# Replacing a hand-ordered attention and feed-forward kernel by a computed order, with w_in in growing chunks and transposes by DMA

## The chip, the cores and the metric

The kernel runs on one core of one Trainium2 chip. The metric is the time of one execution in microseconds (us), taken on the device. It is about 2 us longer than the span of the profile, which runs from the first to the last instruction (before: 236.56 us of time, 234.5 us of span). Each run carries a state, fast or slow; only fast runs are compared, and a profile of a slow run is marked where it is used.

## The reference

Linear attention with a decay per head, in blocks of 64 positions, then a feed-forward block on every token. Shapes: q, k, v are 4 x 8 x 768 x 64 (batch, heads, positions, width), float32; w_in is 512 x 2048, w_out 2048 x 512; the output is 3072 x 512.

```python
for b in range(nb):                                   # 12 blocks of 64 positions
    intra = np.einsum('bhic,bhjc->bhij', qb, kb) * Dmask[None]
    intra = np.einsum('bhij,bhjd->bhid', intra, vb)
    inter = np.einsum('bhid,bhde->bhie', qb * lam_pow[None], kv_state)
    out[:, :, sl] = intra + inter
    kv_state = lam_block[None, :, None, None] * kv_state + np.einsum('bhsd,bhse->bhde', kb_dec, vb)
...
h = x @ w_in
s = np.sin(alpha * h)
g = h + s * s / (alpha + 1e-09)
return (g @ w_out).astype(np.float32)
```

## The kernel before

The kernel cuts the attention into 24 units (256 positions of 4 heads of one batch). A unit loads three tiles of 256 KB (q, k, v), casts and scales them to bf16, transposes q and k on TensorE (eight 128x128 transposes), and then does on TensorE the scores, the masked output, the new states, and the product with the old state ("inter"). Four units make a group of 512 tokens. A group then costs 128 feed-forward matmuls of 128x512: 64 with w_in (tile `hps`, later `gall`) and 64 with w_out (tile `ops`, later `ob`). There are six groups.

The order is written by hand: eight units first, then the feed-forward of group 0, then units and feed-forward work mixed.

```python
    for u in range(8):
        load(u)                                  # SyncE: q, k, v of the first 8 units
    ...
    def group(g, tag):
        n0 = 4 * g
        okv = None
        for n in range(n0, n0 + 4):
            nxt = n + 1 < 8
            if nxt:
                scale_q(n + 1, V)
                scale_k(n + 1, G)
            if n >= WIN0 and n < WIN0 + WCH:     # WIN0 = 5: w_in waits for unit 5
                load_w_in(n - WIN0)
            okv = new_okv()
            if n > 0:
                intermm(n - 1, okv)
                outmm(n - 1, okv)
            scores(n)
            domask(n)
            kvmm(n, okv)
            ...
            if nxt:
                transposes(n + 1, tag, True)     # TensorE, for every unit
                cast_v(n + 1, A)
            busy(NB)                             # 4 dummy matmuls
    ...
    group(0, "hps")
    ...
    group(1, "hps")
    ...
    alone(NFC, hook0, (V, A, V, A, G, A, V, G))  # feed-forward of group 0
    alone(NPRE, hook1)
    ...
    for n in range(8, NU + 4):                   # steady stage: one unit, 8 blocks of 4 matmuls
        macro(n, 4 if n >= 12 else NFC // 4 - NPRE // 4, mid2, late2)
```

Of the kernel before, what the change touches and what calls it, by code (L numbers as in the profile page):

```python
# [12 lines left out]
ET = mybir.EngineType  # L14
# [3 lines left out]
def kernel(  # L18
# [24 lines left out]
    RING = 8  # L43
    WIN0 = 5
    GATE = 8
    N0 = 28
    NB = 4
    NPRE = 8
# [3 lines left out]
    wpool = ctx.enter_context(tc.tile_pool(name="wts", bufs=1))  # L52
    stagep = ctx.enter_context(tc.tile_pool(name="stage", bufs=RING))
    work = ctx.enter_context(tc.tile_pool(name="work", bufs=3))
    kvp = ctx.enter_context(tc.tile_pool(name="kv", bufs=2))
    xtp = ctx.enter_context(tc.tile_pool(name="xt", bufs=3))
    gbp = ctx.enter_context(tc.tile_pool(name="gb", bufs=3))
    mlps = ctx.enter_context(tc.tile_pool(name="mlps", bufs=3))
    outp = ctx.enter_context(tc.tile_pool(name="outp", bufs=3))
    PS = bass.MemoryType.PSUM  # L60
    ps = ctx.enter_context(tc.tile_pool(name="ps", bufs=1, space=PS))

    ctx.enter_context(tc.manual_schedule())


# [7 lines left out]
    BUFS = {"s0": 1, "s1": 1, "okv": 1, "hps": 3, "ops": 1}  # L73
    stage = {}

    def load(u, after=None):
        _, tp, b, _, hh = where(u)
        st = []
        for nm, src in (("q", q), ("k", k), ("v", v)):
            tl = stagep.tile([P, HH, 2, D], FP32, name=f"st_{nm}")  # L80
            ld = nc.sync.dma_start(  # L81
                out=tl[:].rearrange("p h two e -> p h (two e)"),
                in_=src[b, hh * HH:(hh + 1) * HH, tp * W:(tp + 1) * W, :]
                .rearrange("h (p two) e -> p h (two e)", two=2))
            if after is not None:
                tc.add_manual_dep(ld.ins, after.ins.name, mybir.DependencyInfo(
                    mybir.DependencyClass.Sync, mybir.DependencyReason.DATA))
                after = None
            st.append(tl)
        stage[u] = st  # L90

    zeros = consts.tile([P, 2 * P], BF16, name="zeros")
    nc.vector.memset(zeros[:], 0.0)
    warm = consts.tile([1, 1], FP32, name="warm")
    nc.vector.memset(warm[:], 0.0)  # L95
    nc.scalar.activation(out=warm[:], in_=warm[:], func=ACTF.Sin)
    lam_bc = consts.tile([P, H], FP32, name="lam_bc")
    nc.sync.dma_start(out=lam_bc[:], in_=lam.partition_broadcast(P))
    alpha_r = consts.tile([NFC, P], FP32, name="alpha_r")
    nc.scalar.dma_start(out=alpha_r[:], in_=moe_alpha.rearrange("(f p) -> f p", p=P))  # L100
    for u in range(8):
        load(u)

# [3 lines left out]
    for c in range(2):  # L107
        sl = slice(c * D, (c + 1) * D)
        nc.gpsimd.iota(out=pos[sl, :], pattern=[[0, 1]], base=1, channel_multiplier=2,
                       allow_small_or_imprecise_dtypes=True)  # L110
        nc.gpsimd.iota(out=jt[sl, :], pattern=[[1, 2]], base=0, channel_multiplier=2,
                       allow_small_or_imprecise_dtypes=True)
    it = consts.tile([P, 2, D], FP32, name="it")
    nc.gpsimd.iota(out=it[:], pattern=[[1, 2], [2, D]], base=0, channel_multiplier=0,
                   allow_small_or_imprecise_dtypes=True)
# [5 lines left out]
    nc.vector.tensor_tensor(  # L121
        out=mask[:], in0=it[:].rearrange("p two e -> p (two e)").unsqueeze(1)
        .to_broadcast([P, 2, 2 * D]),
        in1=jt[:].unsqueeze(2).to_broadcast([P, 2, 2 * D]), op=ALU.is_ge)
    E = consts.tile([P, 2, H], FP32, name="E")
    R = consts.tile([P, 2, H], FP32, name="R")
    nc.gpsimd.tensor_tensor(out=E[:, 0], in0=lam_bc[:], in1=pos[:].to_broadcast([P, H]),
                            op=ALU.pow)

    LT = consts.tile([P, H], FP32, name="LT")  # L130
    nc.vector.tensor_tensor(out=LT[:], in0=lam_bc[:], in1=lam_bc[:], op=ALU.mult)
    for i in range(6):
        nc.vector.tensor_tensor(out=LT[:], in0=LT[:], in1=LT[:], op=ALU.mult)
    nc.vector.tensor_tensor(out=E[:, 1], in0=E[:, 0], in1=lam_bc[:], op=ALU.mult)
    nc.vector.reciprocal(out=R[:], in_=E[:])
# [3 lines left out]
    w_in_sb = wpool.tile([P, NDC, DFF], BF16, name="w_in_sb")  # L139
    w_out_sb = wpool.tile([P, NFC, DM], BF16, name="w_out_sb")  # L140
    WCH = 4

    def load_w_in(j):
        w = DFF // WCH
        nc.gpsimd.dma_start(
            out=w_in_sb[:, :, j * w:(j + 1) * w],
            in_=moe_w_in[:, j * w:(j + 1) * w].rearrange("(c p) g -> p c g", p=P))

    def load_w_out(j):
        n = NFC // WCH  # L150
        nc.gpsimd.dma_start(
            out=w_out_sb[:, j * n:(j + 1) * n, :],
            in_=moe_w_out[j * n * P:(j + 1) * n * P, :].rearrange("(f p) d -> p f d", p=P))

    cast = {}

    def scale_q(u, eng):
        hh = where(u)[4]
        QL = work.tile([P, 2, HH, D], BF16, name="QL")
        hs = slice(hh * HH, (hh + 1) * HH)  # L160
        eng.tensor_tensor(out=QL[:], in0=stage[u][0][:].rearrange("p h two e -> p two h e"),  # L161
                          in1=E[:, :, hs].unsqueeze(3).to_broadcast([P, 2, HH, D]),
                          op=ALU.mult)
        cast[u, "q"] = QL

    def scale_k(u, eng):
        hh = where(u)[4]
        KD = work.tile([P, 2, HH, D], BF16, name="KD", bufs=4)
        hs = slice(hh * HH, (hh + 1) * HH)
        eng.tensor_tensor(out=KD[:], in0=stage[u][1][:].rearrange("p h two e -> p two h e"),  # L170
                          in1=R[:, :, hs].unsqueeze(3).to_broadcast([P, 2, HH, D]),
                          op=ALU.mult)
        cast[u, "k"] = KD

    def cast_v(u, eng):
        VB = work.tile([P, 2, HH, D], BF16, name="VB", bufs=4)
        v_in = stage[u][2][:].rearrange("p h two e -> p two h e")
        if eng is nc.scalar:
            nc.scalar.copy(out=VB[:], in_=v_in)  # L179
        else:  # L180
            eng.tensor_copy(out=VB[:], in_=v_in)
        cast[u, "v"] = VB

    qkt = {}

    def transposes(u, tag="s0", split=False):
        QT = work.tile([P, 2, 2, 2, P], BF16, name="QT")
        if split:
            pts = [ps.tile([P, 2, 2, P], BF16, name="pt", tag=tag, bufs=BUFS[tag])
                   for j in range(2)]  # L190
        else:
            pt = ps.tile([P, 2, 2, 2, P], BF16, name="pt", tag=tag, bufs=BUFS[tag])
            pts = [pt[:, 0], pt[:, 1]]
        for j, key in ((0, "q"), (1, "k")):
            for hp in range(2):
                for par in range(2):
                    nc.tensor.transpose(out=pts[j][:, hp, par, :],  # L197
                                        in_=cast[u, key][:, par, 2 * hp:2 * hp + 2, :],
                                        identity=iden[:])
        if split:  # L200
            nc.scalar.copy(out=QT[:, 1], in_=pts[1][:])  # L201
            nc.vector.tensor_copy(out=QT[:, 0], in_=pts[0][:])
        else:
            nc.scalar.copy(out=QT[:], in_=pt[:])  # L204
        qkt[u] = QT

    half = [slice(0, D), slice(D, 2 * D)]
    stm = {}
    sps = {}

    def scores(u):
        QT = qkt[u]
        sp = [ps.tile([P, 2, 2, P], FP32, name="sp", tag=f"s{hd}", bufs=1)
              for hd in range(2)]
        for hp in range(2):
            for par in range(2):
                for c in range(2):
                    for hd in range(2):
                        nc.tensor.matmul(  # L219
                            out=sp[hd][half[c], par, hp, :],  # L220
                            lhsT=QT[half[hd], 1, hp, par, half[c]],
                            rhs=QT[half[hd], 0, hp, :, half[c]],
                            start=True, stop=True)
        sps[u] = sp

    def domask(u):
        sp = sps.pop(u)
        ST = work.tile([P, 2, 2, 2, P], BF16, name="ST")
        for hd in range(2):
            nc.vector.tensor_tensor(  # L230
                out=ST[:, hd], in0=sp[hd][:],
                in1=mask[:].unsqueeze(2).to_broadcast([P, 2, 2, P]), op=ALU.mult)
        stm[u] = ST

    kv = {}
    kvold = {}

    def kvmm(u, okv):
        _, tp, b, _, hh = where(u)
        KD, VB = cast[u, "k"], cast[u, "v"]  # L240
        nch = 2 if tp < 2 else 1
        for par in range(2):
            for hp in range(2):
                for c in range(nch):
                    for hd in range(2):
                        h = 2 * hp + hd
                        nc.tensor.matmul(  # L247
# [4 lines left out]

    kva = {}

    def kv_copy(u, okv):

        _, tp, b, _, hh = where(u)
        nch = 2 if tp < 2 else 1
# [222 lines left out]
    def macro(n, nf, mid=None, late=None):  # L481
# [18 lines left out]
        if mid:  # L500
            mid(n)
# [81 lines left out]
```

## Time and profile before

| | before |
|---|---|
| time, median of 3 runs | 236.56 us (236.48 to 236.93) |
| span of the profiled run | 234.5 us |
| TensorE busy | 213.9 us, 91% |
| first feed-forward matmul | 31.84 us |
| last TensorE instruction | 229.6 us |

The page of before. The first line is each engine's busy time. The next lines cut the span into 40 slices of 5.9 us: TensorE's busy share in tenths, its granted clock, and the DMA engines' share and throughput. Then come the queue that SyncE issues to (packets, MB, share of the span of 16 DMA engines) and the chain of waits.

```profile
PE 213.9 (91%) x2166; PEld 113.9 (49%) x2189; DVE 154.4 (66%) x261; ACT 131.6 (56%) x216; POOL 115.5 (49%) x182
...
PE   8687689968899999999999999999999999998991
...
PEclk9999999997999999999999999999999999999999
DMA  5999899999846555534633633621122022210333
GB/s 153 296 291 290 148 181 184 207 180 268 236 124 179 155 156 157 150 77 137 178 70 113 180 101 90 173 45 25 22 48 45 0 48 45 45 43 13 82 67 67
...
q1 hardware_dynamic: 42000, 25.18, 41.8%
...
PE 71%; SPq 7%; DVE 6%; POOL 4%; issue 4%; ACT 4%; DMA 2%; POOLq 0%; ACTq 0%
```

Read from it: TensorE is full from the twelfth slice on (64 us), so time can be won before that (the low digits) and by giving TensorE less to do. The DMA engines are busy up to about 64 us as well (digits of 8 and 9 after the first slice; 290 GB/s from 6 to 23 us, 148 to 268 after that), then about half used.

TensorE's timeline of before (start, duration, line, operation, count, and in brackets the idle time before it and who ended it):

```profile
31.26 0.42 PE L313 MATMUL okv<-ST,VB 64*64 64x128 bf16 x16
31.84 14.00 PE L342 MATMUL hps<-xt,w_in_sb 128*128 128x512 bf16 x62 [0.16 <-issue]
46.23 4.53 PE L342 MATMUL hps<-xt,w_in_sb 128*128 128x512 bf16 x20 [0.40 <-DVE gall L356]
53.66 0.59 PE L197 MATMUL pt<-iden,QL 128*128 128x128 bf16 x4 [2.90 <-DVE gall L356]
```

The feed-forward starts at 31.84 us, when all eight units are done. The wait of 2.90 us ends at VectorE, which spent 3.40 us on one square at 48.77 us (the median of its squares is 0.42). VectorE's timeline of before:

```profile
48.77 3.40 DVE L355 TENSOR_TENSOR s_1127<-s_1125 128x512 bf16<-128x512 bf16 x1
```

**Lost TensorE time.** A busy share hides how much of the busy time was needed, because matmuls at half clock count as busy too, and because the profile models where matmuls end (it draws a 128x512 feed-forward matmul 0.38 us long, while they start 0.2163 us apart). So I use another measure throughout, and work it out from the traces: lost time at t is t minus the needed work of all matmuls started by t. Needed work is a matmul's spacing in undisturbed stretches of these traces: 0.2163 us for a 128x512 feed-forward matmul, 0.245 us for 16 of the 64x64 attention matmuls, 0.0535 us for an inter matmul, 0.0575 us for a transpose. (Starts are taken from the weight loads, since a few per cent of matmul records are missing: 364 of the 384 `hps` matmuls of before are recorded, and all 384 of their weight loads.) Before has 198.1 us of needed work and has lost 21.0 us at its first feed-forward matmul, 26.4 us at 60 us, and 31.5 us at the end; then 4.9 us pass from the last matmul to the end of the span: 198.1 + 31.5 + 4.9 = 234.5.

### The profile page before, as it was taken

To read this page: it belongs to the slowest core of one execution; us is meant where nothing else is said; L and a number is where in the kernel's file an instruction comes from. 1 tells how busy PE (TensorE), PEld (TensorE's weight loads), DVE (VectorE), ACT (ScalarE), POOL (GpSimd) and SP (SyncE) were. 2 spreads that over 40 slices of the span, in tenths; PEclk is the share of its full clock that TensorE was granted. 3 is DMA by queue.
4 is the path that set the end of the run, shared out by engine and by line. 5 is a ranking of instruction groups with operands and counts; after the bars stand their busy time and mean duration, and the time that the engine had idled before them with its cause. 6 is when DMAs were issued, how large, how long until landed. Compare 5 with 4: busy or idle time off the path is not lost.

```text
span 234.5 us, 5410 instructions
## 1 busy us (share of the span) xinstructions
PE 213.9 (91%) x2166; PEld 113.9 (49%) x2189; DVE 154.4 (66%) x261; ACT 131.6 (56%) x216; POOL 115.5 (49%) x182
## 2 busy tenths in 40 slices
PE   8687689968899999999999999999999999998991
PEld 5465544324455554555555455455455444443440
DVE  3887948997766556686686687677668756765000
ACT  2466669966755755665646656556565535453110
POOL 5568976980989997855854642651511000000000
PEclk9999999997999999999999999999999999999999
DMA  5999899999846555534633633621122022210333
GB/s 153 296 291 290 148 181 184 207 180 268 236 124 179 155 156 157 150 77 137 178 70 113 180 101 90 173 45 25 22 48 45 0 48 45 45 43 13 82 67 67
DMA packets 46281, 29.72 MB, mean 127 GB/s; under 512 B 2208, under 2 KB 43184, under 8 KB 46256
## 3 DMA queue, kind: packets, MB, share of 16 engines
q1 hardware_dynamic: 42000, 25.18, 41.8%
q0 software_dynamic: 4224, 4.19, 11.8%
q8 instruction: 17, 0.28, 0.5%
q14 instruction: 8, 0.07, 0.1%
q10 hardware_dynamic: 32, 0.01, 0.0%
HBM read 27.28 MB, written 6.29 MB: 143 GB/s over the span
## 4 chain that ended last, share of the span: by engine, by line
PE 71%; SPq 7%; DVE 6%; POOL 4%; issue 4%; ACT 4%; DMA 2%; POOLq 0%; ACTq 0%
PE ops L369 35%; PE hps L342 26%; SPq L81 7%; PE pt L197 3%; PE sp L219 2%; DMA st_k<-in_k_dram 2%; DVE gall L356 2%; PE okv L313 2%; PE okv L298 2%; DVE s_1127 L355 1%; DVE QL L161 1%; ACT xt L324 1%; PE okv L247 1%; ACT ob L376 1%; POOL KD L170 1%
## 5 line engine op out<-in xcount | busy, mean ns | idle before, releaser
L342 PE MATMUL hps<-xt,w_in_sb 128*128 128x512 bf16 x364 | 94.8, 383 | 3.1 <-ACT xt L324 1.2
L369 PE MATMUL ops<-w_out_sb,gall 128*128 128x512 bf16 x381 | 94.6, 379 | 0.9 <-ACT ob L376 0.7
L342 PEld LDWEIGHTS <-w_in_sb 128*128 128x128 bf16 x384 | 36.4, 99 | 44.7 <-issue 4.5
L369 PEld LDWEIGHTS <-gall 128*128 128x128 bf16 x384 | 36.9, 98 | 42.6 <-issue 1.0
L230 DVE TENSOR_TENSOR ST<-sp,mask 128x512 bf16<-128x512 f32 x48 | 30.8, 682 | 1.5 <-PE sp L219 1.2
L170 POOL TENSOR_TENSOR KD<-st_k,R 128x512 bf16<-128x512 f32 x24 | 26.4, 1099 | 5.7 <-DMA st_k<-in_k_dram 5.1
L204 ACT COPY QT<-pt 128x1024 bf16<-128x1024 bf16 x16 | 16.2, 1012 | 21.9 <-PE pt L197 21.9
L376 ACT COPY ob<-ops 128x512 f32<-128x512 f32 x24 | 14.0, 585 | 19.1 <-PE ops L369 19.1
L324 ACT CAST xt<-okv 128x512 bf16<-128x512 f32 x24 | 14.1, 587 | 6.1 <-PE okv L247 5.2
L161 POOL TENSOR_TENSOR QL<-st_q,E 128x512 bf16<-128x512 f32 x16 | 17.4, 1088 | 0.0
L197 PE MATMUL pt<-iden,QL 128*128 128x128 bf16 x96 | 9.6, 223 | 4.8 <-DVE gall L356 2.9
L197 PE MATMUL pt<-iden,KD 128*128 128x128 bf16 x96 | 9.6, 224 | 3.5 <-POOL KD L170 3.4
L197 PEld LDWEIGHTS <-QL 128*128 128x128 bf16 x96 | 6.8, 99 | 9.7 <-issue 4.1
L179 ACT CAST VB<-st_v 128x512 bf16<-128x512 f32 x14 | 8.6, 616 | 5.1 <-DMA st_v<-in_v_dram 5.1
L419 PE MATMUL bz<-zeros 128*128 128x256 bf16 x60 | 10.3, 326 | 1.1 <-DVE warm L95 1.1
L219 PE MATMUL sp<-QT 64*64 64x128 bf16 x384 | 9.9, 221 | 0.7 <-ACT QT L201 0.7
L313 PE MATMUL okv<-ST,VB 64*64 64x128 bf16 x384 | 9.8, 218 | 0.0
L197 PEld LDWEIGHTS <-KD 128*128 128x128 bf16 x96 | 6.3, 100 | 4.7 <-POOL KD L170 4.7
L161 DVE TENSOR_TENSOR QL<-st_q,E 128x512 bf16<-128x512 f32 x8 | 7.8, 970 | 1.0 <-DMA st_q<-in_q_dram 0.9
L419 PEld LDWEIGHTS <-zeros 128*128 128x128 bf16 x60 | 6.5, 117 | 2.7 <-DVE warm L95 1.1
L219 PEld LDWEIGHTS <-QT 64*64 64x64 bf16 x384 | 6.4, 106 | 2.9 <-ACT QT L201 0.8
L247 PE MATMUL okv<-VB,KD 64*64 64x64 bf16 x320 | 7.2, 193 | 0.3
(531 smaller groups left out, 316.5 us busy)
## 6 DMA issues: line engine op xcount, KB each, us to landing
st_q<-in_q_dram SPq DMA_DIRECT2D x24, 256.0 KB, 4.0
st_k<-in_k_dram SPq DMA_DIRECT2D x24, 256.0 KB, 4.6
st_v<-in_v_dram SPq DMA_DIRECT2D x24, 256.0 KB, 5.1
out_dram<-ob SPq DMA_DIRECT2D x48, 128.0 KB, 2.4
w_in_sb<-in_moe_w_in_dram POOLq DMA_DIRECT2D x4, 512.0 KB, 6.5
w_out_sb<-in_moe_w_out_dram POOLq DMA_DIRECT2D x4, 512.0 KB, 8.1
lam_bc<-in_lam_dram SPq DMA_DIRECT2D x1, 4.0 KB, 3.0
alpha_r<-in_moe_alpha_dram ACTq DMA_DIRECT2D x1, 8.0 KB, 2.9
```

The lines of the kernel that those rows point to most:

```text
L81: ld = nc.sync.dma_start(out=tl[:].rearrange("p h two e -> p h (two e)"), in_=src[b, hh * HH:(hh + 1) * HH, tp * W:(tp + 1) * W, :] .rearr ...
L161: eng.tensor_tensor(out=QL[:], in0=stage[u][0][:].rearrange("p h two e -> p two h e"), in1=E[:, :, hs].unsqueeze(3).to_broadcast([P, 2, HH ...
L170: eng.tensor_tensor(out=KD[:], in0=stage[u][1][:].rearrange("p h two e -> p two h e"), in1=R[:, :, hs].unsqueeze(3).to_broadcast([P, 2, HH ...
L197: nc.tensor.transpose(out=pts[j][:, hp, par, :], in_=cast[u, key][:, par, 2 * hp:2 * hp + 2, :], identity=iden[:])
L204: nc.scalar.copy(out=QT[:], in_=pt[:])
L219: nc.tensor.matmul(out=sp[hd][half[c], par, hp, :], lhsT=QT[half[hd], 1, hp, par, half[c]], rhs=QT[half[hd], 0, hp, :, half[c]], start=Tru ...
L230: nc.vector.tensor_tensor(out=ST[:, hd], in0=sp[hd][:], in1=mask[:].unsqueeze(2).to_broadcast([P, 2, 2, P]), op=ALU.mult)
L324: nc.scalar.copy(out=xt[g][:, 2 * hh:2 * hh + 2, bb, :, :].rearrange("p hp c i -> p c hp i"), in_=okv[:, :, 0:2 * P].rearrange("p c (hp i) ...
L342: f1mm[g, f] = nc.tensor.matmul(out=hps, lhsT=w_in_sb[:, c, f * P:(f + 1) * P], rhs=xt[g][:, c].rearrange("p b c i -> p (b c i)"), start=( ...
L369: f2mm[:] = [nc.tensor.matmul(out=ops[:], lhsT=gall[g][:, f, m * P:(m + 1) * P], rhs=w_out_sb[:, f, :], start=(f == 0), stop=(f == NFC - 1))]
L376: nc.scalar.copy(out=ob[:], in_=ops[:])
L419: nc.tensor.matmul(out=bz[:], lhsT=zeros[:, :P], rhs=zeros[:], start=True, stop=True)
```

## The change

Intent: a small planner in Python (a list scheduler with a model of DMA time) orders all operations instead of the hand. With that come these changes:

- w_in in six growing chunks, the first issued behind the third unit's scaling of v, so that the feed-forward of group 0 can start long before eight units are done.
- The first states go to two of the four PSUM banks that the feed-forward uses later; VectorE decays one there directly, instead of a copy and a chain on GpSimd.
- Transposes of units 8 to 23 leave TensorE: SyncE issues them as DMA transposes, SBUF to SBUF.
- q is no longer scaled at its cast; the scale moves into the eviction of the attention output. Squares leave VectorE: 73 on ScalarE, 23 on GpSimd.
- Output stores, loads and DMA transposes all go through SyncE's queue, in the planner's order. A load has the priority number of its unit minus 200, a transpose minus 400, an output store minus 6; the lower number goes first among those that the planner holds ready.

The diff, cut to its core (nearly every line of the kernel moved):

```diff
-    RING = 8
-    WIN0 = 5
+    RING = 7
+    WI = (128, 128, 256, 512, 512, 512)
+    WG = (2, 3, 3, 3, 4, 4)
+    WH = (4, 5, 6, 7)
...
+class Plan:
+    BEGIN, LAND, DEPTH = {"SP": 1.0, "POOL": 1.4}, 1.7, 6
...
+    def turn_dma(op, u):
+        T[u, "qt"] = slot(op, work, "qt", [P, 2, 2, 2, P], BF16)
+        SY.dma_start_transpose(
+            out=T[u, "qt"][:].rearrange("p j par hp i -> p (j par hp) i"),
+            in_=T[u, "qk"][:].rearrange("p j par h e -> p (j par h e)"))
...
+            oo = add(f"ld{u}{'qkv'[i]}", on("SP", 0.5), [gate], vtl,          # vtl = vt_unit(u) - 200
+                     ..., dma=(.87, .027), gives={"st": 3}, lag=0.05, ...)
...
+        if early:                                    # units 0 to 7: TensorE, as before
+            tq = add(f"tq{u}", on("PE", .22), [cq], b4 - 6, lambda op: turn_pe(op, u, 0), ...)
+        else:                                        # units 8 to 23
+            dt = add(f"dt{u}", on("SP", .4), [cq, ck], b4 - 400, lambda op: turn_dma(op, u),
+                     take=("qt",), give=((cq, "qk"),), dma=(.9, .027))
...
+            d0 = add(f"bx{u}", on("DVE", .45), [kvm, tb0], b4 - 1, lambda op: decay_first(op, kvm, u),
+                     give=((kvm, "f"),))
...
+        st = add(f"out_{g}_{m}", on("SP", 1.0), [ev], vt - 6, lambda op: f2st(op, ev, g, m),
+                 give=((ev, "ob"),), dma=(.65, .08))
...
-    for n in range(8, NU + 4):
-        macro(n, 4 if n >= 12 else NFC // 4 - NPRE // 4, mid2, late2)
+    for op in plan.run():
+        op.emit(op)
```

`dma=(.9, .027)` on the transpose is what the planner believes a transpose costs the DMA engines: 0.9 us, about the same as a load of the same 256 KB (0.87).

## The prediction

> What bounds the kernel now: TensorE, 213.9 of 234.5 us busy (91%, busy table), 71% of the chain of waits. From the spacing in the timeline, a 128x512 feed-forward matmul costs 0.216 us, so 768 of them are 166 us; a unit's attention matmuls (scores, masked output, states, inter) cost about 1.0 us, 24 units 24 us; the eight transposes of a unit 0.47 us, 24 units 11 us. That is 201 us of needed work. The other 33 us:
> - 0 to 31.8 us: the first feed-forward matmul starts at 31.8, after all 8 first units. Only 8 x 1.47 = 12 us of it is needed work: 20 us lost. Loads pace the units (three of 256 KB, 0.87 us apart, so 2.6 us per unit); w_in is first issued at 24.1 us.
> - 50.8 to 57 us: TensorE waits 2.9 us for VectorE (a square of 3.4 us and the combine behind it); the table of windows shows the granted clock at 0.50 from 54 to 56 us, another 2 us lost. [...]
> - 229.8 us to the end: last eviction and store, 4.7 us.
> - 59 to 229.8 us: 168 us of work in 171 us.
>
> What the change does.
> 1. Transposes of units 8 to 23 go from TensorE to DMA: 16 x 0.47 = 7.5 us off the critical engine. Added: 16 DMA transposes of 256 KB, whose cost no trace here shows; DMA is 13 to 47% busy after 100 us, and each is issued well ahead.
> 2. Feed-forward of group 0 starts after units 0 to 3 plus the scores and state of unit 4 (order of instructions on TensorE), with w_in chunk 0 issued after unit 2. About 16 loads x 0.87 us, two small chunks and landing put that near 19 us (estimate), with about 7 us of needed work before: 12 us lost instead of 20. Gain 8 us.
> 3. Then DMA rules: 8 units 21 us, w_in about 11 us, w_out about 10 us (estimates from the load spacing and issue-to-landing of 6.5 us per 1 MB chunk) end near 44 to 46 us. [...] I allow 2 to 4 us of lost TensorE time here, against 5 before. Gain about 2 us.
> 4. Squares leave VectorE for ScalarE (73) and GpSimd (23); Q scaling moves into the output eviction. Estimated busy: VectorE 128, ScalarE 150, GpSimd about 115 us, all under TensorE's 195. The 2.9 us wait should vanish.
> 5. The tail is unchanged.
>
> Sum: 8 + 2 + 7.5, so 236.6 - 18 = 218 us. Range 212 to 226. Faster by over 2%: 0.96; within 2%: 0.03; slower: 0.01.
>
> What would show it: first feed-forward matmul at 17 to 21 us; no TensorE wait over 2 us after it and no granted clock of 0.5; TensorE ends about 5 us before the span; unit period in the steady stage about 8.0 us, not 8.4.
>
> Against it: slow DMA transposes, or SyncE's in-order queue held by a transpose's wait delaying loads and stores; w_out later than planned, stalling TensorE between 38 and 55 us; 39 warm-up matmuls at the half clock delaying unit 0; ScalarE at 70% becoming the pace of the first feed-forward stage.

The sum came to 8 + 2 + 7.5 = 17.5 us, taken off 236.6 us as 18, so 218 us. The end of stage 3 "near 44 to 46 us" adds the times of loads, w_in and w_out as if they shared the DMA engines; in this text that is the author's estimate, and what after measured of it stands under "Why the prediction was wrong". The warm-up matmuls that it fears "at the half clock" are read from the trace of before: they start 0.213 us apart up to 5.5 us and 0.109 us apart after that.

## The result, and the profile after

| | before | after |
|---|---|---|
| time, median of 4 runs | 236.52 us (236.09 to 236.93) | 229.47 us (227.55 to 232.16, one of them slow) |
| ratio of fast runs, after to before | | 0.9674 [0.9631, 0.9718] |
| span of the profiled run | 234.5 us | 227.5 us |
| first feed-forward matmul | 31.84 us | 22.41 us |
| last TensorE instruction | 229.6 us | 222.2 us |
| needed TensorE work | 198.1 us | 190.7 us |
| lost TensorE time, whole run | 31.5 us | 31.5 us |

A ratio is the mean time of one kernel's fast runs over the mean of the other's fast runs of the same rounds, so it is not quite the ratio of the medians that are quoted. The three fast runs of after have a median of 229.27 us.

The change is faster by 7 us, not by the 18 that I predicted, and the result lies above the predicted range. The lower rows say where: the whole gain is as large as the 7.4 us of transposes taken from TensorE. The lost time, on which I had expected to win 10 us, is the same in both kernels as a whole; where it lies differs, as the table further down shows.

The page of after, the same lines:

```profile
PE 208.3 (92%) x2015; PEld 107.4 (47%) x2041; DVE 123.3 (54%) x205; ACT 144.0 (63%) x254; POOL 123.2 (54%) x202
...
PE   8698888979899949999999999999999999999990
...
PEclk9955899999999996999999999999999999999998
DMA  5999999999999999997877721420221022220442
GB/s 138 291 284 248 228 213 216 220 255 236 227 283 229 292 221 314 191 291 171 166 196 145 105 53 43 92 49 1 46 49 39 8 50 46 46 43 3 95 91 48
...
q1 hardware_dynamic: 58752, 29.37, 59.2%
...
PE 63%; DMA 22%; SPq 6%; POOL 4%; ACT 1%; issue 1%; DVE 0%; ACTq 0%
```

Three things are new. TensorE has a hole in the fifteenth slice (the 4, at 80 to 85 us). DMA is full not until about 64 us but until about 100 us, and holds 22% of the chain of waits instead of 2%. SyncE's queue moved 29.37 MB instead of 25.18 (the sixteen transposes) and took 0.592 x 227.5 = 134.7 us of the 16 engines instead of 98.0: 36.7 us more, at most 2.3 us for each transpose, against the 0.9 us that the planner reckoned with. That is an upper limit: counted by packet size in the packed trace, the transposes' own packets (256 bytes) took 28.2 us, 1.8 us for each, and the packets of a 256 KB load, on the same scale, 1.1 us in after and 1.0 in before.

TensorE's timeline of after, at the start of the feed-forward and at the hole:

```profile
22.01 0.61 PE L376 MATMUL pt<-iden,qk 128*128 128x128 bf16 x4
22.41 0.63 PE L544 MATMUL hps<-xt,w_in_sb 128*128 128x512 bf16 x1
...
80.72 0.39 PE L501 MATMUL okv<-qt,kvbd 128*128 128x128 bf16 x4
84.23 0.42 PE L399 MATMUL sp<-qt 64*64 64x128 bf16 x16 [3.12 <-DMA qt<-qk]
...
85.15 2.65 PE L572 MATMUL ops<-w_out_sb,gall 128*128 128x512 bf16 x7 [0.16 <-issue]
87.59 2.64 PE L544 MATMUL hps<-xt,w_in_sb 128*128 128x512 bf16 x8
```

The scores of unit 12 wait 3.12 us for the unit's DMA transpose (`qt<-qk`). After that eight feed-forward matmuls take 2.64 us, where eight take 1.89 us elsewhere.

The table of windows of after (from:to and width, busy us and instructions of TensorE, its weight loads, VectorE, ScalarE and GpSimd, then granted clock, DMA share, GB/s; the share adds up the time of all packets over 16 engines, so it exceeds 1 where packets overlap):

```profile
10.00:20.00 10.00, 8.44 (x193) 6.32 (x193) 6.99 (x13) 6.34 (x17) 7.65 (x11) 0.53 1.23 286
20.00:30.00 10.00, 8.63 (x133) 5.35 (x133) 7.57 (x14) 8.24 (x17) 7.51 (x9) 0.79 1.26 219
...
85.00:90.00 5.00, 4.85 (x15) 1.93 (x17) 1.67 (x3) 0.96 (x2) 3.75 (x7) 0.66 1.17 296
```

Two stretches run below full clock: about 11 to 24 us, and behind the wait at 84 us.

Why the transpose was late, from SyncE's timeline of after (each row is one instruction of its queue, with the time that it took to issue):

```profile
63.78 2.01 SPq L388 DMA_TRANSPOSE qt<-qk  x1
65.83 0.58 SPq L344 DMA_DIRECT2D st_v<-in_v_dram  x1
...
75.45 0.83 SPq L344 DMA_DIRECT2D st_k<-in_k_dram  x1
76.32 2.36 SPq L344 DMA_DIRECT2D st_v<-in_v_dram  x1
79.22 2.10 SPq L388 DMA_TRANSPOSE qt<-qk  x1
```

and from GpSimd's timeline of after, the cast that completes the transpose's input:

```profile
73.77 0.61 POOL L360 CAST qk<-st_k 128x512 bf16<-128x512 f32 x1
```

The input was ready at 74.4 us, the transpose was issued at 79.22 and landed about 5 us later. Between the transpose of unit 11 and that of unit 12 stand 13 loads in SyncE's order (the expectations below say 14), at 0.5 to 2.4 us each.

Lost TensorE time, as defined above, in us:

| | at the first feed-forward matmul | at 50 | at 60 | at 80 | at 90 | at the end |
|---|---|---|---|---|---|---|
| before | 21.0 (at 31.8 us) | 21.6 | 26.4 | 27.4 | 27.8 | 31.5 |
| after | 15.8 (at 22.4 us) | 22.3 | 23.1 | 24.3 | 29.2 | 31.5 |

After is 5 us ahead when its feed-forward starts, but by 50 us that lead is gone (22.3 against 21.6). It is 3 us ahead from 60 to 80 us, because before loses 4.8 us between 50 and 60 us, where TensorE waits for VectorE, and after only 0.8. It gives back more than these at 80 to 90 us. So three questions stood: what sets the first 22 us, what the loss from 22 to 50 us is, and what makes the loss at 80 to 90 us.

### The profile page after: what moved, and what is told of

It is laid out like the page before. It is cut to its first block, busy times and chain, and to the rows that moved or that the text cites. A ratio compares the mean times of both kernels' runs of the same rounds, so it can differ in the third digit from the quotient of the medians.

```text
span 227.5 us, 5158 instructions
## 1 busy us (share of the span) xinstructions
PE 208.3 (92%) x2015; PEld 107.4 (47%) x2041; DVE 123.3 (54%) x205; ACT 144.0 (63%) x254; POOL 123.2 (54%) x202
## 3 DMA queue, kind: packets, MB, share of 16 engines
q1 hardware_dynamic: 58752, 29.37, 59.2%
## 4 chain that ended last, share of the span: by engine, by line
PE 63%; DMA 22%; SPq 6%; POOL 4%; ACT 1%; issue 1%; DVE 0%; ACTq 0%
PE ops L572 30%; PE hps L544 27%; DMA qt<-qk 6%; SPq L344 6%; DMA st_k<-in_k_dram 5%; DMA st_v<-in_v_dram 5%; DMA w_in_sb<-in_moe_w_in_dram 5%; PE sp L399 2%; POOL vb L366 1%; PE okv L514 1%; PE okv L501 1%; POOL qk L360 1%; PE okv L429 1%; POOL w_in_sb L327 1%; ACT s L551 1%
## 5 line engine op out<-in xcount | busy, mean ns | idle before, releaser
L563 DVE SCALAR_TENSOR_TENSOR gall<-s,r_sb,hps 128x512 bf16<-128x512 bf16 x96 | 70.9, 746 | 64.5 <-ACT s L558 47.9
L551 ACT ACTIVATE s<-hps,alpha_sb 128x512 bf16<-128x512 f32 x96 | 65.3, 686 | 45.1 <-PE hps L544 44.3
L558 ACT ACTIVATE s<-s 128x512 bf16<-128x512 bf16 x73 | 46.0, 630 | 2.1
L560 POOL TENSOR_TENSOR s<-s 128x512 bf16<-128x512 bf16 x23 | 23.9, 1040 | 42.7 <-ACT s L551 42.7
L408 DVE TENSOR_TENSOR sm<-sp,mask 128x512 bf16<-128x512 f32 x48 | 32.3, 683 | 7.5 <-PE sp L399 7.5
L366 POOL TENSOR_TENSOR vb<-st_v,R 128x512 bf16<-128x512 f32 x24 | 25.1, 1046 | 6.7 <-DMA st_v<-in_v_dram 3.7
L454 POOL TENSOR_TENSOR kvx<-kva,kvs 128x128 f32<-128x128 f32 x32 | 14.6, 456 | 20.8 <-ACT kva L439 20.6
L457 POOL TENSOR_TENSOR kvbd<-kvx,LBD 128x256 bf16<-128x256 f32 x32 | 19.6, 614 | 4.5 <-PE okv L501 2.1
L531 DVE TENSOR_TENSOR xt<-okv,ET 128x512 bf16<-128x512 f32 x24 | 16.4, 685 | 6.1 <-PE okv L514 5.9
L360 POOL CAST qk<-st_k 128x512 bf16<-128x512 f32 x19 | 11.6, 612 | 1.1 <-DMA st_k<-in_k_dram 1.1
## 6 DMA issues: line engine op xcount, KB each, us to landing
w_out_sb<-in_moe_w_out_dram POOLq DMA_DIRECT2D x4, 512.0 KB, 15.3
```

What stands on the lines that cost most here:

```text
L360: ENGINE[op.eng].tensor_copy(out=o, in_=i)
L366: ENGINE[op.eng].tensor_tensor(out=T[u, "vb"][:], in0=T[u, "v"][:].rearrange("p h two e -> p two h e"), in1=R[:, :, hs].unsqueeze(3).to_br ...
L408: V.tensor_tensor(out=T[u, "sm"][:, hd], in0=T[u, "sp"][hd][:], in1=mask[:].unsqueeze(2).to_broadcast([P, 2, 2, P]), op=ALU.mult)
L457: G.tensor_tensor(out=bd[:], in0=X.unsqueeze(2).to_broadcast([P, 2, 2, D]), in1=LBD[:, hs, :].unsqueeze(3).to_broadcast([P, 2, 2, D]), op= ...
L531: V.tensor_tensor(out=xt[g][:, 2 * hh:2 * hh + 2, bb, :, :].rearrange("p hp c i -> p c hp i"), in0=T[u, "op"][:, :, 0:2 * P].rearrange("p ...
L551: A.activation(out=op.tile[:, cols], in_=mm.tile[:, cols], func=ACTF.Sin, scale=alpha_sb[:, f:f + 1])
```

## The experiments

Theories. QUEUE: SyncE's queue works in order (the transpose of unit 12, ready at 74.4 us, was issued at 79.22, behind the loads ahead of it), and loads issued far ahead keep an urgent transpose behind them. CLOCK: the half clock at 11 to 24 us costs the start. LOADS: the bytes to be loaded set the start. Rivals to each are in the expectations. All edits are against the kernel after unless said otherwise. "Before" was timed again (medians 235.79 to 236.39 us).

| run | median us (range) | ratio to before [95%] |
|---|---|---|
| e1_fill | 229.21 (228.87 to 230.96) | 0.9745 [0.9693, 0.9796] |
| e2_ring4 | 225.26 (224.74 to 226.36) | 0.9578 [0.9529, 0.9626] |
| e3_dt_r5 | 224.64 (224.24 to 225.15) | 0.9537 [0.9500, 0.9574] |
| e4_peturn | 231.42 (231.09 to 231.61) | 0.9822 [0.9786, 0.9858] |
| e5_third (wrong result) | 220.13 (219.79 to 220.59) | 0.9315 [0.9287, 0.9342] |
| e6_even | 226.64 (225.77 to 226.72) | 0.9580 [0.9553, 0.9607] |
| e7_decay | 224.40 (223.94 to 224.54) | 0.9490 [0.9468, 0.9513] |
| e8_fill2 | 224.39 (224.12 to 224.71) | 0.9494 [0.9472, 0.9516] |
| e9_price | 235.04 (232.48 to 237.03; two fast, two slow) | 0.9864 [0.9828, 0.9899] |
| e10_ring5 | 227.51 (226.54 to 228.70) | 0.9631 [0.9594, 0.9669] |
| e11_r4dt | 223.40 (223.22 to 224.01) | 0.9460 [0.9440, 0.9479] |
| e12_wh | 225.88 (225.82 to 226.21) | 0.9563 [0.9547, 0.9578] |
| e13_price_st | 224.18 (223.66 to 224.32) | 0.9480 [0.9462, 0.9499] |
| e14_after_st | 231.14 (230.55 to 233.14) | 0.9794 [0.9744, 0.9843] |
| e15_r4dt_st | 224.10 (223.88 to 224.21) | 0.9480 [0.9464, 0.9496] |
| e16_r5dt_st | 223.86 (223.65 to 224.12) | 0.9472 [0.9451, 0.9492] |

### e1_fill: four dummy matmuls ahead of each transpose group (eight per unit) at the start

```diff
+        if 1 <= u <= 5:
+            bz = bank(op, "f", [P, 2 * P], FP32, "bz")
+            for _ in range(4):
+                nc.tensor.matmul(out=bz[:], lhsT=zeros[:, :P], rhs=zeros[:], start=True, stop=True)
```

> Adds 40 warm-up matmuls (4 ahead of each transpose group of units 1 to 5) and changes nothing else in any engine's order. Theory CLOCK: the new order has no fillers between units, TensorE falls to the half clock from about 11 to 23 us, and this delays the first feed-forward matmul (22.4 us). Then the granted clock in 10 to 20 us goes from 0.53 to 1.0, the first feed-forward matmul starts near 20.5 us, and the kernel gains 2 to 4 us (near 226.5). Rival LOADS: the units are paced by their loads (2.6 us each), the half clock only fills time that was idle; then the clock is restored but the first feed-forward matmul stays within 0.5 us of 22.4 and the time stays within 1 us of 229.5.

229.21 us. The granted clock was 1.00 in both windows from 10 to 30 us, but the feed-forward started at 24.1 us instead of 22.4 (four dummies take 0.61 us in its trace, the eight of a unit 1.2; that this is what delayed it was not shown), and lost time at 50 us stayed 22.3. That spoke against CLOCK without killing it; e8 repeats it with fewer dummies.

### e2_ring4: four input buffers instead of seven

```diff
-    RING = 7
+    RING = 4
```

> Load buffers per tensor 7 to 4, so loads run at most 4 units ahead. Theory PREFETCH: the 3.1 us wait of unit 12's scores at 81 us (and the half clock after it, 4.9 us lost together from 80 to 90) comes from 14 loads that the queue puts between the transposes of units 11 and 12, which fill the 16 DMA engines and SyncE's in-order queue. Then that wait falls below 1 us and the time to about 225. Rival VOLUME: the bytes needed by 80 us plus the cost of the transposes fill the DMA engines anyway; then a wait of 2 us or more stays or moves to another unit, and the time stays at 228 to 231. Second risk: units 4 to 7 load later, which would show as a later first feed-forward matmul.

225.26 us, 4 us below after. Lost time is 24.6 at 80 us and 24.8 at 90: the loss of 4.9 us at 80 to 90 us is gone, as QUEUE expects. Fewer input buffers made the kernel faster.

### e3_dt_r5: the planner's price of a transpose 2.2 us, ring of five

```diff
-                     take=("qt",), give=((cq, "qk"),), dma=(.9, .027))
+                     take=("qt",), give=((cq, "qk"),), dma=(2.2, .027))
-    RING = 7
+    RING = 5
```

> The schedule's own DMA price of one transpose raised from 0.9 to 2.2 us (from the trace: 36.7 us more queue time over 16 transposes, 2.3 us each) and load buffers 5. Theory PRICE: the planner believed the transposes cheap and put too much in front of them; with the right price 5 loads lie between the transposes of units 11 and 12 in place of 14, the wait at unit 12 goes and the time is 224 to 226.5. Rival VOLUME: the DMA engines stay full until 95 us and the order of the queue does not matter; time within 1 us of 229.5.

224.64 us. The price is only a number in the planner; apart from one square that moved from GpSimd to ScalarE, only the order and the number of input buffers changed. TensorE's timeline of e3_dt_r5 at unit 12 has no wait, and behind it no half clock (eight matmuls in 1.89 us):

```profile
79.61 0.39 PE L501 MATMUL okv<-qt,kvbd 128*128 128x128 bf16 x4
79.92 0.42 PE L399 MATMUL sp<-qt 64*64 64x128 bf16 x16
...
83.22 1.89 PE L544 MATMUL hps<-xt,w_in_sb 128*128 128x512 bf16 x8
```

In SyncE's timeline of e3_dt_r5 the transpose of unit 12 now stands five loads behind the one of unit 11 rather than 13, and is issued 6.4 us earlier than in after (1.6 us of that because its input was ready earlier, at 72.8 us, and 4.8 us because no load stood in front of it any more once the input was ready):

```profile
65.58 1.51 SPq L388 DMA_TRANSPOSE qt<-qk  x1
...
72.81 1.26 SPq L388 DMA_TRANSPOSE qt<-qk  x1
```

The part from the start to 50 us is untouched (lost time 22.3). What of this is the ring and what the price, e9 and e10 ask.

### e4_peturn: all transposes back on TensorE

```diff
-            dt = add(f"dt{u}", on("SP", .4), [cq, ck], b4 - 400, lambda op: turn_dma(op, u), ...)
+            tq = add(f"tq{u}", on("PE", .22), [cq], b4 - 6, lambda op: turn_pe(op, u, 0), ...)
+            e0, tk, e1 = ...                      # as for the units 0 to 7
-                     ... bufs=8 if c == 0 else 2
+                     ... bufs=8 if c == 0 else 4  # which the new order needs
```

> Units 8 to 23 are transposed on TensorE again, with the evictions on VectorE or ScalarE, all else planned as before (one more pair of small state buffers, which the new order needs). Adds 16 x 0.46 = 7.4 us of TensorE work. If the DMA transposes are what fills the DMA engines and stalls unit 12, lost time falls by about 5 us and the time is 231 to 233 (so the DMA transposes are worth only 2 to 3 us net). If loads alone fill them, the stall stays and the time is 236 or more (DMA transposes worth 7 us). No wait on a DMA transpose can remain; the DMA share from 60 to 95 us should drop below 1.0.

231.42 us. Needed work is 198.1 us again and there is no loss at 80 to 90 us (24.7, then 24.4). So the DMA transposes gave 7.4 us of TensorE work but in after's order were worth 2 us (231.42 against 229.47 by medians; 3.5 by the ratios 0.9822 and 0.9674). Against e3_dt_r5 they are worth 6.8 us: once they are issued in time, nearly all of the 7.4.

### e5_third: one third of the input bytes of units 0 to 7 left out

Based on e3_dt_r5. The result is wrong (v is replaced by k).

```diff
+        if i == 2 and u < 8:
+            T[u, "v"] = T[u, "k"]
+            return
```

> Wrong result on purpose. e3 with the v loads of units 0 to 7 left out (their k tile is used in its place), so 2.1 MB or about 7 us less for the DMA engines in the first 30 us; every engine instruction is kept. Theory LOADS: the first feed-forward matmul (22.4 us in e3) and the 22 us of TensorE time lost by 50 us are set by the bytes that must land. Then the first feed-forward matmul comes 3 us or more earlier, the lost time at 50 us falls by 4 us or more, and the kernel is at or below 221. Rival CHAIN: the units are paced by their own chain of casts, transposes, copies and masks (3.3 us a unit); then the first feed-forward matmul stays within 1 us of 22.4, and any gain comes only after 30 us, from w_in and w_out landing sooner.

220.13 us, 4.5 us below e3_dt_r5 by medians (5.2 by the ratios). Lost time at 50 us fell from 22.3 to 18.0. The first feed-forward matmul moved from 22.4 to only 20.7, between what LOADS and its rival expected. So bytes count: the eight loads left out (8 x 0.87 = 7 us of DMA) are worth 4.3 of the 22.3 us lost up to 50 us. The moment of the first feed-forward matmul says less. In the profiles of the fifteen kernels that keep all bytes and the growing chunks (after among them) it lies anywhere from 20.9 us (e4) to 24.1 us (e1), while the lost time at 50 us stays at 22.1 to 22.6. So the shift of 1.7 us in e5 need not come from bytes, and what sets the rest of the 22.3 us I did not split further.

### e6_even: w_in in four equal chunks

Based on e3_dt_r5.

```diff
-    WI = (128, 128, 256, 512, 512, 512)
-    WG = (2, 3, 3, 3, 4, 4)
+    WI = (512, 512, 512, 512)
+    WG = (2, 3, 3, 4)
```

> e3 with w_in in four equal chunks of 512 columns again, in place of 128, 128, 256 and three of 512, still behind units 2 and 3. Undoes one named part of the change. Theory: the first chunk of 1 MB lands 2 to 3 us later than one of 256 KB, the first feed-forward matmul moves from 22.4 to 24 us or later, and the kernel loses 0.5 to 2 us. If the start is bound elsewhere the time is within 0.5 us of e3 (224.6).

226.64 us against 224.64 (ratios 0.958 and 0.9537): the growing chunks are worth 1 to 2 us. TensorE's timeline of e6_even shows its first feed-forward matmul, 0.8 us later than in e3_dt_r5 and held up by the first chunk (e3_dt_r5 waits for w_in as well, three times and 2.1 us in all, but later):

```profile
23.14 0.61 PE L544 MATMUL hps<-xt,w_in_sb 128*128 128x512 bf16 x1 [1.04 <-DMA w_in_sb<-in_moe_w_in_dram]
```

### e7_decay: first states decayed on GpSimd again

Based on e3_dt_r5.

```diff
-            d0 = add(f"bx{u}", on("DVE", .45), [kvm, tb0], b4 - 1, ...)       # VectorE, from PSUM
+            d0 = add(f"bx{u}", on("POOL", .6), [kc, tb0], b4 - 1, ...)        # GpSimd, from the copy
```

> e3 with the first states of units 0 to 7 decayed by GpSimd from the copy that ScalarE makes, as in the kernel before, in place of VectorE reading the spare PSUM banks. Undoes the other named part. Theory: adds a hop (0.5 us copy, then 0.6 us on GpSimd behind casts) to each unit before its inter matmuls; first feed-forward matmul 1 us later, time 0.5 to 2 us more than e3. Rival: the state is not what the units wait for; no change within 0.5 us.

224.40 us, no slower than 224.64, although the first feed-forward matmul came at 23.4 us. The part that the change names last, states decayed by VectorE from PSUM, is worth nothing here: lost time at 50 us is 22.6 against 22.3.

### e8_fill2: two dummy matmuls ahead of each transpose group (four per unit)

Based on e3_dt_r5; the edit of e1_fill with `range(2)`.

> e3 with 2 in place of 4 fillers ahead of each transpose group of units 1 to 5 (e1 used 4, about 1.2 us a unit, which may itself have delayed the units). If CLOCK has any share in the start, the granted clock is 1.0 from 10 to 20 us and the first feed-forward matmul comes at 21 us or before, 1 us or more gained on e3. If LOADS or CHAIN alone set it, the time is within 0.5 us of e3.

224.39 us. The table of windows of e8_fill2 has the full clock:

```profile
10.00:20.00 10.00, 8.46 (x221) 5.57 (x210) 7.74 (x14) 7.72 (x20) 8.33 (x11) 1.00 1.29 279
20.00:30.00 10.00, 8.77 (x157) 5.14 (x159) 7.74 (x14) 8.29 (x17) 6.28 (x8) 1.00 1.23 222
```

The first feed-forward matmul (22.8 us), the lost time at 50 us (22.3) and the time did not improve. CLOCK falls: as much was lost by 50 us at a granted clock of 1.00 as in e3_dt_r5 (22.3 us), where it was 0.59 from 10 to 20 us and 0.90 from 20 to 30.

### e9_price: the price alone

```diff
-                     take=("qt",), give=((cq, "qk"),), dma=(.9, .027))
+                     take=("qt",), give=((cq, "qk"),), dma=(2.2, .027))
```

> The price alone: the planner reckons a DMA transpose at 2.2 us of DMA instead of 0.9, the input ring stays at 7. Theory ORDER (the loss at 80 to 90 us comes from where SyncE's queue places the transpose of unit 12 among the loads; a right price places it better): 224.3 to 226.0 us, lost TensorE time no higher at 90 us than 1 us above that at 80. Theory DEPTH (a ring of 7 lets loads crowd the transposes out whatever the price): 228 to 230.5 us with the loss still there.

Both theories missed. The two fast runs took 232.48 and 233.63 us, slower than after. The profile is of a slow run (237.03 us), so it is read for the mechanism and not for the size. No TensorE wait on a transpose is left in it, as ORDER expects. But a new loss of 11 us lies between 95 and 115 us (26.3, then 37.4). TensorE's waits in e9_price (total us, times, longest us):

```profile
PE hps L544 <- DVE gall L563: 5.6, 6, 2.2
...
PE ops L572 <- ACT ob L578: 1.3, 1, 1.3
```

ScalarE's timeline of e9_price shows the evictions of finished outputs (`ob`): three by 59 us, which fill all three output buffers, then none for 50 us.

```profile
59.15 0.58 ACT L578 COPY ob<-ops 128x512 f32<-128x512 f32 x1 [0.28 <-PE ops L572]
...
109.20 1.06 ACT L578 COPY ob<-ops 128x512 f32<-128x512 f32 x2
```

SyncE's timeline of e9_price shows why; this row is the first output store:

```profile
101.97 2.47 SPq L585 DMA_DIRECT2D out_dram<-ob  x4
```

A store has the lowest priority in the planner's order for SyncE, and with dearer transposes the planner found loads to put ahead of it until 102 us. As long as no output buffer is free, a finished `ops` tile keeps one of the four PSUM banks that `hps` also needs. But GpSimd was 97% busy from 50 to 110 us in the same profile, and that was a rival. e13 decides.

### e10_ring5: the ring alone

```diff
-    RING = 7
+    RING = 5
```

> The ring alone: 5 input buffers instead of 7, price left at 0.9. Theory DEPTH: 224.3 to 226.0 us, no loss at 80 to 90 us. Theory ORDER with the price as what matters: between 226.5 and 230 us, a wait of TensorE over 2 us on a DMA transpose somewhere between 70 and 100 us.

227.51 us, between the two. Two TensorE waits on transposes remain, of 2.0 us together and at most 1.3. So the ring of 5 mends part, and price and ring together (224.64) mend the rest; a ring of 4 mends all of it without the price (e2); the price alone does harm.

### e11_r4dt: ring of four and the price

```diff
-    RING = 7
+    RING = 4
...
-                     take=("qt",), give=((cq, "qk"),), dma=(.9, .027))
+                     take=("qt",), give=((cq, "qk"),), dma=(2.2, .027))
```

> Ring of 4 and the price of 2.2 together. If the stall was all that either of them mends, 224.2 to 225.6 us like the ring of 5 with the price (224.6). If fewer loads in flight also helps the start, below 223.8; if the ring of 4 starves units in the steady stage, above 226.

223.40 us, the best of all runs with a right result. Lost time is 22.1 at 50 us and 24.1 at 90. The first store comes at 69.67 us in SyncE's timeline of e11_r4dt:

```profile
69.67 2.46 SPq L585 DMA_DIRECT2D out_dram<-ob  x4
```

### e12_wh: w_out issued earlier

Based on e3_dt_r5.

```diff
-    WH = (4, 5, 6, 7)
+    WH = (4, 5, 5, 6)
```

> Ring of 5, price 2.2, and the chunks of w_out issued earlier by a unit (behind units 4, 5, 5, 6 rather than 4, 5, 6, 7). If w_out still paces TensorE between 24 and 50 us, 222.5 to 224.0 us and lost time at 50 us about 1 us lower than 22.3. If it is the total of bytes that paces that stretch, 224.2 to 225.5 and the lost time at 50 us within 0.5 of 22.3.

225.88 us, not faster than 224.64. Lost time at 50 us is 22.3, as before the edit. The total of bytes paces this stretch, not which bytes come first: w_out came sooner, and the rest later. The time is just above what this side expected, because the order after 80 us changed too (lost time 27.0 at 110 us against 25.2 in e3_dt_r5).

### e13_price_st: the price, and stores ahead of loads

```diff
-                     take=("qt",), give=((cq, "qk"),), dma=(.9, .027))
+                     take=("qt",), give=((cq, "qk"),), dma=(2.2, .027))
...
-        st = add(f"out_{g}_{m}", on("SP", 1.0), [ev], vt - 6,
+        st = add(f"out_{g}_{m}", on("SP", 1.0), [ev], vt - 400,
```

> Price 2.2, ring 7, and output stores ranked ahead of loads in SyncE's queue. If the late stores (first at 102 us in e9_price) held the PSUM banks and caused its loss: first store before 70 us, no loss at 95 to 115 us, 223 to 226 us. If GpSimd's backlog (97% busy from 50 to 110 us) caused it: the loss stays, 230 to 236 us.

224.18 us against 232.5 to 233.6 for e9_price's fast runs: 8 us or more from one number, the rank of the stores. SyncE's timeline of e13_price_st begins its stores at 59.66 us:

```profile
59.66 1.18 SPq L585 DMA_DIRECT2D out_dram<-ob  x2
62.36 2.46 SPq L585 DMA_DIRECT2D out_dram<-ob  x4
```

The loss at 95 to 115 us is gone (24.7 at 100 us, 25.1 at 120). GpSimd was about as busy as in e9 (57.2 of the 60 us from 50 to 110 us). So the late stores made e9's loss, and GpSimd did not. That the unfreed PSUM banks are the link between is read from the code and the waits; no run isolates it.

### e14_after_st: stores ahead of loads, nothing else

The last edit of e13 alone.

> After's price and ring, stores ahead of loads alone. If after's loss at 80 to 90 us comes only from the transpose of unit 12 behind the loads: 228 to 231 us with that wait still there (2 us or more on a DMA transpose). If stores take part: below 227 us.

231.14 us: not better than after. SyncE's timeline of e14_after_st still has loads ahead of the transpose of unit 12:

```profile
65.15 2.64 SPq L388 DMA_TRANSPOSE qt<-qk  x1
...
78.27 0.77 SPq L344 DMA_DIRECT2D st_v<-in_v_dram  x1
79.16 2.79 SPq L388 DMA_TRANSPOSE qt<-qk  x1
```

and TensorE's timeline of e14_after_st the same wait, longer:

```profile
84.66 0.64 PE L399 MATMUL sp<-qt 64*64 64x128 bf16 x16 [4.60 <-DMA qt<-qk]
```

So late stores take no part in after's loss at 80 to 90 us. With e2, e3 and e11 (and e10 in part) that loss is shown to come from the place of the transposes among the loads.

### e15_r4dt_st and e16_r5dt_st: stores ahead of loads, with the price and rings of 4 and 5

> Ring 4, price 2.2, stores ahead of loads. e11_r4dt, which has its first store at 70 us and no loss there, is at 223.4. If nothing is left to gain after 50 us: 222.8 to 224.0. A gain below 222.5 would mean that late stores still cost something at ring 4; above 224.5 that stores ahead of loads delay the loads.

> Ring 5, price 2.2, stores ahead of loads: like e3_dt_r5 (224.6, first store at 84 us) with the stores early. 223.0 to 224.2 if the late stores cost e3 about 1 us against e11; 224.4 to 225.2 if they cost nothing.

224.10 and 223.86 us. Nothing below 222.5 was found: with the transposes in time, early stores gain little at ring 5 (223.86 against 224.64) and nothing at ring 4 (224.10 against 223.40). Eight variants now lie between 223.4 and 225.3 us; what is left of them is the needed work, the start, and the tail.

## Why the prediction was wrong

The prediction was a sum. In terms of the span it was 193.5 us of needed work, 12 lost before the feed-forward, 2 to 4 in the stage where DMA rules, about 3 in the steady stage and 4.7 of tail: about 216 us, or 218 us of time. Measured, in the same terms (profile of after):

| term | predicted | measured | |
|---|---|---|---|
| needed TensorE work | 193.5 | 190.7 | right: 7.4 us less than before; I had counted both 3 us too high |
| lost before the first feed-forward matmul | 12, at 19 us | 15.8, at 22.4 us | mis-sized |
| lost from there to 50 us | 2 to 4 | 6.5 | mis-sized |
| lost at 80 to 90 us | 0 | 4.9 | step failed |
| lost elsewhere (50 to 80, 90 to the end) | about 3 | 4.3 | about right |
| tail | 4.7 | 5.3 | right |

Point by point:

1. *Transposes to DMA.* "7.5 us off the critical engine" was right (7.4). The failed step is the clause behind it: "DMA is 13 to 47% busy after 100 us, and each is issued well ahead." Seven of the sixteen are issued between 49 and 91 us, when DMA is full (a share of 1.15 from 50 to 110 us in after), and the one of unit 12 was issued only about 2 us before TensorE had come to it, behind 13 loads in SyncE's queue. That cost a wait of 3.12 us and the half clock behind it: 4.9 us. Among what would speak against me I named SyncE's in-order queue, but the wrong way round: I feared a transpose delaying loads, and it was loads that delayed a transpose. e2, e3, e11 and e13 show it by removing the loss (e10 in part), e4 by leaving out the transposes, e14 by keeping the loss when only stores are moved.
2. *The start.* The feed-forward did start before all eight units were in, but 15.8 us were lost by then instead of 12, so the lead was 5.2 us instead of 8. The step "Gain 8 us" failed in a second way: the lead did not last. At 50 us after has lost 22.3 us and before 21.6. I had counted an earlier first matmul as a gain, while what is lost by 50 us stayed at 22.1 to 22.6 us wherever that matmul came, and fell only when bytes were taken away (e5: 18.0). My fear of the half clock came true in the profile (0.53) but cost nothing (e8).
3. *The stage where DMA rules.* I allowed 2 to 4 us and measured 6.5 up to 50 us; before loses 5.4 from its first feed-forward matmul to 58 us (4.8 of them after 50 us, at the wait for VectorE), so there was no gain here instead of 2. e5 (fewer bytes) lowers what is lost by 50 us and e12 (same bytes in another order) does not. I had ended this stage "near 44 to 46 us", counting eight units, w_in and w_out. The last chunk of w_out landed at 53.7 us, the loads of units 8 to 20 and seven transposes landed by 100 us, and the DMA row of the page stays full until then. The transposes have no part in the 6.5 us: the first was issued at 49.55 us.
4. *VectorE's wait.* Right: the wait of 2.90 us is gone, and no TensorE wait over 1.5 us except the one on the transpose is left. Of all that I expected to win in lost time, this is what came: 4.0 us between 50 and 60 us.
5. *Steady stage and tail.* Right: the scores of two consecutive units start 7.93 us apart (97.46 and 105.39 us; predicted about 8.0), and the tail is 5.3 us.

So the 11 us that I was wrong by are 4.9 of the missed wait behind SyncE's queue, 7.3 of the two terms of the start that I sized too small (3.8 and 3.5), and about 2 of the rest and the tail, less the 2.8 that I had counted too much of needed work, which hid part of the error by luck. Undoing the first accounts for most of the way to 223.4 us (e11); removing bytes as well as mending the order gives 220.1 (e5, against 224.6 for e3).

What the runs show of the clock and of the DMA engines. The waits of 3.12 us (after) and 2.90 us (before) were each followed by matmuls at half rate (granted clock 0.50 from 86 to 88 us and 0.50 from 54 to 56 us); behind the wait of 4.60 us in e14, 16 scores matmuls took 0.64 us, against 0.42 at 91.45 us of the same trace. At the start of after the clock fell without such a wait (see the last section). And the loads were slower beside w_in and w_out: in after, loads landed 0.90 us apart while they ran alone (from 5.2 to 14.2 us), and 3.65 us apart (from 28.0 to 42.6 us) while chunks of w_in and w_out came in through GpSimd's queue. (The page's median landing of a w_out chunk, 15.3 us against 8.1 in before, is no sign of it: three chunks stood behind others of their own queue, and the last, alone in it, took 8.0.)

What stays open: how the 22.3 us lost by 50 us divide between bytes and the chain of casts, transposes and evictions (e5 shows 4.3 for a third of the input bytes of eight units); and whether a second queue for the transposes or stores would do better than a good order in one.

## What to carry to other kernels

When work moves from the engine that is the bottleneck to DMA, price it by what it costs the DMA engines in the stage where it runs (here 1.8 us of packet time for each transpose, in a stage with a DMA share of 1.15), not on average, and ask what stands ahead of it in the queue that issues it: here one queue kept an urgent transpose behind prefetches for 4.8 us after its input was ready (after), and the stores that free output buffers until 102 us (e9). Prefetching deeper can then be slower (here 229.27 us with seven input buffers, the fast runs of after, and 225.26 with four), and a computed order has to be checked against a trace: here raising one price alone made things worse until the stores' priority was mended too, while fewer input buffers mended the loss without any new price. To size a gain at the start, count lost time on the bottleneck against needed work, up to the point where DMA is no longer full, rather than the moment at which the first main-stage instruction starts.

## What else the traces show of the hardware

- Landing of DMA transposes. Of the six transposes of 256 KB that landed among loads between 55 and 90 us of after, four landed 0.8 to 0.9 us behind the load before them, which is the loads' own spacing of 0.9, and two 2.4 us. By the time of their packets they were dearer, 1.8 us against 1.1 for a load. The sixteen took 3.0 to 9.4 us from issue to landing (median 4.3).
- Transposes on TensorE or by DMA. The eight pipelined transposes of a unit cost TensorE 0.46 us, and the worth of moving them depended on the queue: 2 to 3.5 us for sixteen units in one order, 6.8 us in another.
- Time to issue. It was not small with the DMA engines full: 13 loads took SyncE 12.9 us to issue (65.8 to 78.7 us), about the 1.0 us apiece at which they landed, and the transpose behind them was issued at 79.2 us although its input was ready at 74.4. Whether SyncE or the full engines set that pace no run separates.
- The clock at the start. In after the granted clock was 0.53 from 10 to 20 us although no TensorE wait at the start was longer than 1.0 us, and four dummy matmuls per unit kept it at 1.00 (e8). What about them did it no run separates. In the same stage before ran at 1.00 with 7.78 of 10 us busy and after at 0.53 with 8.44 (some of it busy only because the clock was halved), so the busy share of the profile did not tell which it would be. The table of windows of before:

```profile
10.00:20.00 10.00, 7.78 (x197) 5.85 (x197) 7.73 (x15) 6.67 (x14) 6.81 (x11) 1.00 1.19 290
```
